# Where kᵀ is turned for two units of a gated linear attention, and when two weight sums are made

## The chip, the cores and the metric

The kernel runs on one core of a Trainium2 chip. The metric is the device time in microseconds of one execution. Its engines are TensorE (matrix products and transposes), VectorE, ScalarE, GpSimd and SyncE (which only issues DMAs); the profile calls them PE, DVE, ACT, POOL and SP. GpSimd and ScalarE can issue DMAs as well. Each engine works through its own queue in order and waits where an input is not there yet.

## The reference

All data is float32. The attention has 4 batches, 8 heads, 768 positions and 48 values a head; its output goes as rows of 384 into a gated MLP with 1536 hidden values.

```python
f = 1.0 / (1.0 + np.exp(-f_logit))
for t in range(S):
    state = f[:, :, t, :, None] * state + np.einsum('bhd,bhe->bhde', k[:, :, t], v[:, :, t])
    y[:, :, t] = np.einsum('bhd,bhde->bhe', q[:, :, t], state)
x = y.transpose(0, 2, 1, 3).reshape(B * S, H * D)
g = x @ w_gate
out = (g * sigmoid(g) * (x @ w_val)) @ w_out
```

## The kernel before

**Units.** The 768 positions are cut into 6 chunks of 128. A unit is one batch in one chunk; units are numbered chunk by chunk, so units 4 to 7 are chunk 1. `attention(u)` is a generator: it makes one unit in steps, and others call its steps in between their own work. In a unit a backward scan (L620) gives the tails of the products of f, k times the tails is `kT` (L570), a forward scan (L648) gives the gates and q times them is `qT`. Scores are products of `kT` and `qT` (L666), masked on VectorE (L681) into `A`; `A`, `v` and the decayed state give `y` (L702 to L727). The new state needs `dS`, products of `v` with `kt` (L747). `kt` is `kT` turned, positions on the partitions.

**Two ways to load.** Early units load rows and turn them on TensorE (L590). The last two units of chunk 1, units 6 and 7, and all later ones load 32-by-32 squares (`by_squares(u)`, four DMAs an input, L447) into rooms that VectorE transposes (L604 for f, L614 for k, L652 for q). In chunks 0 and 1 the rooms lie over the raw tiles of the early units, one room for each input, and units 6 and 7 fill theirs from GpSimd's queue; later chunks load from SP's. `load_after(u, what)` issues the loads of the next unit as soon as a room is free.

**Two ways to turn kT.** Without `turned`, four TensorE transposes (L670) into PSUM and a ScalarE copy (L679) make `kt`. With it (chunks 3 and 4 before), VectorE transposes `kT` block by block into the k room, called `beside` there (L636), four DMAs write it to a tile in DRAM (L639), and one DMA reads it back in the other order (L677). There is one `kt` tile.

**The MLP.** Chunk 0's MLP is plain (L802 for gate and value, L825 for the down product) with four PSUM banks in turn; VectorE multiplies in L816. Chunk 1's attention is dealt out between its pieces, and joins of w_out and sums of weights on VectorE go in there too. From chunk 1 on the MLP saves products by sums: a hidden triple makes 15 products (L1004) out of weights and sums, with ScalarE copies (L1009) and VectorE sums (L905, L908) behind each, then seven down products (L1103, L1166) with w_out's quarters and three sums of them, `down_sums`, made once.

**What sets the order.** Up to the first pieces of chunk 0's MLP, and from chunk 1's MLP on, the instructions keep the order in which they are written on each engine (`in_order`). In between, in the rest of chunk 0's MLP with chunk 1's attention, the framework's scheduler chooses by the order written and its own estimate of times; only loads of squares on GpSimd are kept in order with each other. From chunk 1's MLP on a planner deals out the rest of the work: each product is deemed to take 0.86 us, and a list `waiting` holds steps with due times. `CHAINS` and `SCORES` give them for attention, `DOWN_SUMS_AT` for the four instructions of `down_weight_sums`, counted from the start of chunk 1's MLP. Steps that are due are written ahead of the next product, in order of their due times. For chunk 2 the second unit's gate transpose is due at 13.2, the first unit's masks at 14, the second unit's at 26.65. A triple is deemed 12.9 long.

The four sums are `ws1 = b12 - b11`, `ws2 = b22 - ws1`, `b12 = b22 - b12` and `ws4 = b21 - ws2`, each 128 x 1152.

Of the kernel before, what the change touches and what calls it, by code (L numbers as in the profile page):

```python
# [290 lines left out]
def short_path(ctx, tc, ident, least, judge, q, k, v, f_logit, moe_w_gate, moe_w_val, moe_w_out, out):  # L291
# [9 lines left out]
    nc = tc.nc  # L301
    B, H, S, D = q.shape
    C = 128
    NCH = S // C
# [11 lines left out]
    SQUARES = 2  # L316
# [84 lines left out]
    def by_squares(u):  # L401
        return u >= SQUARES * B - 2
# [6 lines left out]
    def v_of(u):  # L409
        return vs[u % (NV if units[u][1] < SQUARES else NV // 2)]  # L410
# [20 lines left out]
    def load(u, what="fkqv"):  # L431
        b, c = units[u]
        rows = slice(c * C, (c + 1) * C)
        inputs = dict(f=f_logit, k=k, q=q, v=v)
        for nm in "fqkv" if c >= SQUARES else "fvkq" if by_squares(u) else "fkqv":
            src = inputs[nm]
            if nm not in what:
                continue
            if nm == "v":
                dst = v_of(u)  # L440
            elif not by_squares(u):
                dst = raw[nm][u % NRAW]
            else:
                since = len(traced)
                for n in range(4):
                    at = Q * (1 - n % 2)
                    (nc.sync if c >= SQUARES else nc.gpsimd).dma_start(  # L447
                        out=rooms[nm][Q * n:Q * (n + 1), at:at + HP * RUN].rearrange("t (a e) -> t a e", a=HP),
                        in_=src[b, n // 2::2, rows, :].rearrange("a (t i) d -> t a (i d)", i=NI))
                if c < SQUARES:  # L450
                    by_pool.extend(ins for ins in traced[since:] if ins.engine == mybir.EngineType.Pool)
                    keep_order(by_pool[-5:])
                continue
            nc.sync.dma_start(out=dst[:, :, 0:D], in_=src[b, :, rows, :].rearrange("h t d -> t h d"))

    def weight_piece(dst, src, parts):

# [80 lines left out]
    def rows_of(par):  # L538
        return slice(W * par, W * par + D)
# [15 lines left out]
    def attention(u):  # L555
        b, c = units[u]
# [5 lines left out]
        in_squares = by_squares(u)  # L562
# [42 lines left out]
            load_after(u, "f")  # L605
        yield

        turned = SQUARES < c < NCH - 1
        kT = att.tile([128, HP, C], FP32, tag="kT", name="kT")
        qT = att.tile([128, HP, C], FP32, tag="qT", name="qT", bufs=2)  # L610
        kp, qp = kT, qT
# [13 lines left out]
        if not in_squares:  # L625
            kp = transposed("kTp", kr)
            qp = transposed("qTp", qr)
            if by_squares(u + 1):
                load(u + 1)
        multiply(kT, kp, pairs(tail, 2)[:, :, 0:C])  # L630
        yield
        if turned:


            beside = rooms["k"][:, 0:HP * C].rearrange("p (i m) -> p i m", i=NI)
            nc.vector.transpose(beside.rearrange("p i (a e) -> p a i e", e=Q), kT.rearrange("p a (i e) -> p a i e", e=Q))  # L636
            turn = turn_pool.tile([Q, NI, HP, NI, Q], FP32, tag="turn", name="turn")
            for r in range(NI):
                nc.sync.dma_start(out=turn[:, :, :, r, :].rearrange("t i a e -> t (i a) e"),  # L639
                                  in_=beside[Q * r:Q * (r + 1)].rearrange("t i (a e) -> t (i a) e", e=Q))  # L640
            load_after(u, "k")
        yield
# [20 lines left out]
        for a in range(HP):  # L663
            for par in range(2):
                r = rows_of(par)
# [8 lines left out]
        if c < NCH - 1:  # L674
            kt = att.tile([128, HP * C], FP32, tag="kt", name="kt")
            if turned:
                nc.sync.dma_start(out=kt, in_=turn.rearrange("t i a r e -> i t (a r e)"))  # L677
            else:
                nc.scalar.copy(kt, p)  # L679
        for par in range(2):  # L680
# [9 lines left out]
        if c and b < B - 1:  # L690
# [8 lines left out]
            for a in range(HP):  # L699
                for par in range(2):  # L700
                    r = rows_of(par)
# [9 lines left out]
            for h in range(H):  # L711
                a, par = h // 2, h % 2
                f = h * D
                while f < (h + 1) * D:
                    n = min((h + 1) * D, (f // 128 + 1) * 128) - f
                    r = W * (a % 2) + f - h * D
                    (nc.gpsimd if c >= SQUARES else nc.sync).dma_start(out=xT[c][f % 128:f % 128 + n, f // 128, b * C:(b + 1) * C],  # L717
                                                                       in_=yT[r:r + n, par, a // 2 * C:(a // 2 + 1) * C])
                    f += n
        else:  # L720
# [15 lines left out]
            for par in range(2):  # L736
                for n in range(DM // Q):
                    h = n // per * 2 + par
# [11 lines left out]
        if c >= SQUARES and u + 2 < len(units):  # L750
            load(u + 2, "v")
# [7 lines left out]
    def load_after(u, what):  # L759

        if u + 1 < len(units) and u + 1 != SQUARES * B:
            load(u + 1, what)

    def attention_steps(c):

        runs = [attention(c * B + b) for b in range(B)]
        order = sorted((2 * b + s, b, n) for b in range(B)
                       for s, n in enumerate((1, 8, 3, 3) if by_squares(c * B + b) else (3, 6, 3, 3)))
        return [lambda b=b, n=n: [next(runs[b]) for _ in range(n)] for _, b, n in order]
# [9 lines left out]
    def keep_order(mine):  # L779
        for a, b in zip(mine, mine[1:]):  # L780
            tc.add_manual_dep(b, a.name, mybir.DependencyInfo(mybir.DependencyClass.NoSync,
                                                              mybir.DependencyReason.DATA), reason="order")
# [115 lines left out]
        return {"o": banks_o, "A": banks_a}[kind].tile([128, 512], FP32, tag=kind, name="sc")  # L898

    FINISH = (3, 5, 6, 7, 9, 10)  # L900
    DOWN_SUMS_AT = (28, 34, 38, 48)
    sums = {}

    def plus(dst, a, b):
# [31 lines left out]
    def down_weight_sums():  # L936

        DH = DM // 2
        b11, b12 = w_out[:, 0:NP, 0:DH], w_out[:, 0:NP, DH:DM]
        b21, b22 = w_out[:, NP:NF, 0:DH], w_out[:, NP:NF, DH:DM]  # L940
        for i in (1, 2, 4):
            down_sums[i] = comb.tile([128, NP, DH], FP32, tag=f"ws{i}", name=f"ws{i}")
        return [lambda: minus(down_sums[1], b12, b11), lambda: minus(down_sums[2], b22, down_sums[1]),
                lambda: minus(b12, b22, b12), lambda: minus(down_sums[4], b21, down_sums[2])]
# [268 lines left out]
    mark = traced[-1]  # L1213
    keep_warm(5)
    first = [attention(b) for b in range(B)]
    done = [0] * B

# [83 lines left out]
    for c in range(2, NCH):  # L1301
        for b in range(B):
            run = attention(c * B + b)
            waiting += [((c - 2) * whole + t, lambda run=run: next(run)) for t in times(c)[b]]
# [4 lines left out]

    waiting += [(at, f) for at, f in zip(DOWN_SUMS_AT, down_weight_sums())]  # L1310
    blocks = {}
# [26 lines left out]
def kernel(  # L1338
# [22 lines left out]
    def judge(bank):  # L1361
# [13 lines left out]
        yield  # L1375

    short_path(tc, ident, least, judge, *args)
    with tc.If(redo[0] > 0, label="redo"):
        general_path(tc, *args)
# [32 lines left out]
```

## Time and profile before

| | |
|---|---|
| median of 3 runs | 604.13 us (604.05 to 604.21) |
| profiled execution | 605.36 us, span of its instructions 603.5 |
| granted TensorE clock | 0.995 |
| L670, transposes of kT on TensorE | 48 in 12 units, 0.27 us each, overlapping |
| L679, their copies on ScalarE | 12, 0.585 us each |
| L636, VectorE's transposes of kT | 8, 0.703 us each |
| L639 and L677, DMAs of the turn, on SP | 32 of 64 KB, 0.626 us to issue, 2.2 to landing; 8 of 256 KB, 0.568 to issue |
| L447, squares on GpSimd | 24 of 96 KB, 0.55 us to issue |
| L454, v of units 5 to 7 on SP | 192 KB each, 0.47 us to issue, 2.7 to landing |
| L908, sums of w_out's quarters | 4 in all, 1.34 us each |

The span runs from the first to the last instruction. A duration in the profile is that of one instruction; instructions of one engine overlap a little, so from start to start it is shorter. The chain of waits follows the work that ended last back to the beginning. In a timeline a line gives start, duration, engine, source line, operation, output and inputs; in brackets stands the idle time ahead of it and what ended it.

### The profile page before, as it was taken

The page shows a single profiled execution, that of the slowest core. Times are in us where ns is not written, and L with a number is a line of the kernel's source. Part 1 is how long each engine was busy: PE and PEld are TensorE (multiplying, and loading weights), DVE is VectorE, ACT ScalarE, POOL GpSimd, SP SyncE. Part 2 cuts the span into 40 slices and gives each one's busy share as a digit, 9 for nine tenths or more (in the row PEclk, how much of TensorE's full clock was granted, in tenths as well). Part 3 has the DMA queues.
Part 4 walks back from the last instruction along what each step waited for, and adds up shares of the span by engine and source line. Part 5 has one row for each costly group of instructions (what it writes and reads, how often), then busy time and mean ns, then how long its engine had stood idle before and what let it go on. Part 6 is the DMA issues. An engine that isn't in the chain of part 4 may idle for free.

```text
span 603.5 us, 10851 instructions
## 1 busy us (share of the span) xinstructions
PE 591.9 (98%) x4004; PEld 487.6 (81%) x4004; DVE 480.3 (80%) x831; ACT 294.8 (49%) x559; POOL 86.2 (14%) x199
## 2 busy tenths in 40 slices
PE   7899999999999999999999999999999999999996
PEld 5754545667888899888899888899988899988896
DVE  7999997868999977998895978995878982666631
ACT  2577853215776521567631476742376730356600
POOL 1001251000030150030330030330030320000000
PEclk9999999999999999999999999999999999999999
DMA  9998682015322044342434333343240100100001
GB/s 197 243 294 286 199 211 63 5 35 157 80 63 69 17 129 124 102 114 65 115 103 109 116 91 71 87 110 101 85 105 26 28 9 6 53 1 1 1 1 55
DMA packets 105210, 56.28 MB, mean 93 GB/s; under 512 B 67136, under 2 KB 97216, under 8 KB 105152
## 3 DMA queue, kind: packets, MB, share of 16 engines
q1 hardware_dynamic: 97632, 46.49, 29.4%
q0 software_dynamic: 5504, 6.30, 3.5%
q10 hardware_dynamic: 2016, 2.75, 1.3%
q8 instruction: 32, 0.52, 0.4%
q14 instruction: 26, 0.21, 0.1%
HBM read 45.74 MB, written 6.82 MB: 87 GB/s over the span
## 4 chain that ended last, share of the span: by engine, by line
PE 93%; DVE 5%; issue 1%; ACT 0%; DVEq 0%; ACTq 0%
PE o L1103 19%; PE A L1004 16%; PE B L1004 13%; PE c L1004 5%; PE o L1004 5%; PE gate L802 5%; PE o L825 5%; PE val L802 5%; PE sc L666 4%; PE o L1166 3%; PE y L706 3%; PE y L727 2%; PE dS L747 2%; PE y L702 2%; PE kt L670 1%; DVE c L908 1%
## 5 line engine op out<-in xcount | busy, mean ns | idle before, releaser
L717 POOL DMA_DIRECT2D xT<-yT x120 | 59.9, 507 | 50.3 <-ACT yT L710 45.3
L1103 PE MATMUL o<-w_out,h 128*128 128x192 f32 x360 | 62.0, 327 | 0.5 <-DVE h L956 0.5
L1004 PE MATMUL A<-xs,w_both 128*128 128x256 f32 x240 | 62.2, 382 | 0.0
L1103 PEld LDWEIGHTS o<-w_out,h 128*128 128x128 f32 x360 | 58.7, 190 | 1.7 <-DVE h L956 0.8
L1009 ACT COPY c<-A 128x512 f32<-128x512 f32 x40 | 23.3, 583 | 59.5 <-PE A L1004 59.5
L1009 ACT COPY aside<-A 128x512 f32<-128x512 f32 x60 | 35.1, 586 | 33.7 <-PE A L1004 33.6
L905 DVE TENSOR_TENSOR c<-c,aside 128x512 f32<-128x512 f32 x60 | 41.1, 685 | 12.4 <-ACT aside L1009 11.0
L1004 PEld LDWEIGHTS A<-xs,w_both 128*128 128x128 f32 x240 | 44.9, 190 | 6.6
L956 DVE TENSOR_TENSOR h<-h,c 128x256 f32<-128x256 f32 x100 | 40.4, 412 | 7.3 <-ACT h L1020 7.1
L681 DVE TENSOR_TENSOR A<-sc,causal 128x512 f32<-128x512 f32 x48 | 30.9, 686 | 16.9 <-PE sc L666 16.9
L908 DVE TENSOR_TENSOR c<-c,aside 128x512 f32<-128x512 f32 x60 | 40.9, 682 | 2.8 <-ACT aside L1009 2.8
L1020 ACT ACTIVATE h<-c 128x256 f32<-128x256 f32 x100 | 39.2, 416 | 7.6 <-DVE c L905 5.7
L656 POOL MEMSET gates<- 128x4 f32 x24 | 3.3, 139 | 272.6 <-DVE qT L570 267.5
L1103 PE MATMUL o<-ws,h 128*128 128x192 f32 x240 | 41.5, 328 | 0.2 <-DVE A L681 0.2
L1004 PE MATMUL B<-xs,w_both 128*128 128x256 f32 x160 | 41.3, 380 | 0.1
L1004 PE MATMUL c<-xT,w_both 128*128 128x256 f32 x160 | 41.2, 380 | 0.1
L1004 PE MATMUL A<-xs,extra 128*128 128x256 f32 x160 | 41.2, 380 | 0.0
L1004 PE MATMUL B<-xT,extra 128*128 128x256 f32 x160 | 41.1, 379 | 0.0
L1009 ACT COPY aside<-B 128x512 f32<-128x512 f32 x60 | 35.1, 585 | 9.5 <-PE B L1004 6.6
L1103 PEld LDWEIGHTS o<-ws,h 128*128 128x128 f32 x240 | 39.1, 190 | 0.8 <-DVE A L681 0.4
L905 DVE TENSOR_TENSOR c<-c,o 128x384 f32<-128x384 f32 x15 | 8.3, 552 | 36.3 <-PE o L1103 36.3
L908 DVE TENSOR_TENSOR c<-o,c 128x512 f32<-128x512 f32 x40 | 27.4, 684 | 11.0 <-ACT h L1020 6.2
(149 smaller groups left out, 1221.0 us busy)
## 6 DMA issues: line engine op xcount, KB each, us to landing
fsquares<-in_f_logit_dram SPq DMA_DIRECT2D x64, 96.0 KB, 2.5
qsquares<-in_q_dram SPq DMA_DIRECT2D x64, 96.0 KB, 2.1
ksquares<-in_k_dram SPq DMA_DIRECT2D x64, 96.0 KB, 2.4
v<-in_v_dram SPq DMA_DIRECT2D x24, 192.0 KB, 2.7
w<-in_moe_w_gate_dram SPq DMA_DIRECT2D x6, 768.0 KB, 6.1
w<-in_moe_w_val_dram SPq DMA_DIRECT2D x6, 768.0 KB, 6.2
w<-in_moe_w_out_dram SPq DMA_DIRECT2D x6, 768.0 KB, 5.6
out_dram<-ob ACTq DMA_DIRECT2D x14, 192.0 KB, 2.0
```

The lines of the kernel that those rows point to most:

```text
L666: nc.tensor.matmul(sc[par][:, a * C:(a + 1) * C], lhsT=kT[r, a, :], rhs=qT[r, a, :], start=True, stop=True)
L681: nc.vector.tensor_tensor(A[:, par], sc[par].rearrange("p (a t) -> p a t", t=C), causal.unsqueeze(1).broadcast_to((128, HP, C)), ALU.mult)
L717: (nc.gpsimd if c >= SQUARES else nc.sync).dma_start(out=xT[c][f % 128:f % 128 + n, f // 128, b * C:(b + 1) * C], in_=yT[r:r + n, par, a / ...
L802: nc.tensor.matmul(p, lhsT=w[:, j, i, :], rhs=xT[c][:, i, :], start=(i == 0), stop=(i == KT - 1))
L825: nc.tensor.matmul(p, lhsT=hidden_tile(h, n // 2)[:, n % 2 * 2 + b // 2, b % 2 * C:(b % 2 + 1) * C], rhs=w_out[:, j, :], start=(n == 0), s ...
L905: nc.vector.tensor_tensor(dst, a, b, ALU.add)
L908: nc.vector.tensor_tensor(dst, a, b, ALU.subtract)
L956: lagging.append(lambda: f(*args))
L1004: nc.tensor.matmul(p[name][:, n, :], lhsT=weights_of[a][:, n, j, :], rhs=tokens[b], start=fresh and n == 0, stop=True, skip_group_check=True)
L1009: nc.scalar.copy(t, p[name])
L1020: nc.scalar.activation(dst, src[:, 0, :], AF.Silu)
L1103: nc.tensor.matmul(p[:, n, :], lhsT=lhsTs[j][:, n * C:(n + 1) * C], rhs=rhs[:, j, :], start=first and j == order[0] and n == 0, stop=j == ...
```

## The change

It does two things. For units 6 and 7 `kT` is turned by VectorE and DRAM, with the DMAs on GpSimd's queue, in place of TensorE's transposes and ScalarE's copy; as the k room then holds `beside`, unit 7's k loads come after unit 6's turn instead of right after its k transpose. The v loads of units 6 and 7 move from SP's queue to GpSimd's. And the first two of the four sums have other due times: `ws1` 13.1 in place of 28, `ws2` 26.5 in place of 34.

```diff
@@ load
-            nc.sync.dma_start(out=dst[:, :, 0:D], in_=src[b, :, rows, :].rearrange("h t d -> t h d"))
+            queue = nc.gpsimd if c < SQUARES and by_squares(u) else nc.sync
+            queue.dma_start(out=dst[:, :, 0:D], in_=src[b, :, rows, :].rearrange("h t d -> t h d"))
@@ attention
-        turned = SQUARES < c < NCH - 1
+        turned = SQUARES < c < NCH - 1 or c < SQUARES and in_squares
+        turn_queue = nc.sync if c >= SQUARES else nc.gpsimd
...
             for r in range(NI):
-                nc.sync.dma_start(out=turn[:, :, :, r, :].rearrange("t i a e -> t (i a) e"),
+                turn_queue.dma_start(out=turn[:, :, :, r, :].rearrange("t i a e -> t (i a) e"),
                                   in_=beside[Q * r:Q * (r + 1)].rearrange("t i (a e) -> t (i a) e", e=Q))
             load_after(u, "k")
...
             if turned:
-                nc.sync.dma_start(out=kt, in_=turn.rearrange("t i a r e -> i t (a r e)"))
+                turn_queue.dma_start(out=kt, in_=turn.rearrange("t i a r e -> i t (a r e)"))
             else:
                 nc.scalar.copy(kt, p)
@@
-    DOWN_SUMS_AT = (28, 34, 38, 48)
+    DOWN_SUMS_AT = (13.1, 26.5, 38, 48)
```

## The prediction

> **What bounds the kernel now.** I read the busy shares first, then the chain of waits, then the two stretches that the change touches as timelines.
>
> ```profile
> PE 591.9 (98%) x4004; PEld 487.6 (81%) x4004; DVE 480.3 (80%) x831; ACT 294.8 (49%) x559; POOL 86.2 (14%) x199
> PE 93%; DVE 5%; issue 1%; ACT 0%; DVEq 0%; ACTq 0%
> ```
>
> TensorE carries 93% of the chain that ended last, VectorE 5%. So TensorE time taken away inside a stretch in which TensorE never waits shortens the kernel one for one; VectorE time counts only where TensorE waits for it. From 46 to 143 us the waits list names none of TensorE's, and in five windows over 30 to 143 it is busy all the time. There the chain reads:
>
> ```profile
> 106.15 1.09 PE sc L666 x16
> 107.83 5.16 PE o L825 x16
> ...
> 123.56 1.09 PE sc L666 x16
> 125.23 5.16 PE o L825 x16
> ```
>
> The first pair is unit 6 (chunk 1, batch 2), the second unit 7. Scores end at 107.24 and 124.65, the next matmuls begin at 107.83 and 125.23: 0.59 and 0.58 us lie between, and what stands in them in the timeline is four transposes of L670.
>
> The second stretch, 143 to 205 us, is chunk 1's MLP with chunk 2's attention. VectorE's timeline:
>
> ```profile
> 156.41 0.68 DVE L905 TENSOR_TENSOR c<-c,aside 128x512 f32<-128x512 f32 x1
> 157.94 1.12 DVE L604 STREAM_TRANSPOSE gates<-fsquares 128x512 f32<-128x512 f32 x1 [0.84 <-issue]
> ...
> 174.29 1.29 DVE L681 TENSOR_TENSOR A<-sc,causal 128x512 f32<-128x512 f32 x2 [1.41 <-PE sc L666]
> ...
> 176.15 1.35 DVE L908 TENSOR_TENSOR ws<-w_out 128x1152 f32<-128x1152 f32 x1
> ...
> 185.92 1.33 DVE L908 TENSOR_TENSOR ws<-w_out,ws 128x1152 f32<-128x1152 f32 x1
> ```
>
> and TensorE's at its end:
>
> ```profile
> 204.90 1.57 PE L1103 MATMUL o<-w_out,h 128*128 128x192 f32 x8 [0.55 <-DVE h L956]
> ```
>
> VectorE has two idle places, 0.84 us before 157.94 and 1.41 us before 174.29, and none from there to 204. The two sums stand behind the second one. TensorE's 15 products of a triple start every 0.863 us; 30 of them from 174.68 should end at 200.58, and the next work starts at 201.59. So 1.01 us is lost, in steps at 188.91, 195.30 and smaller ones, and 0.55 more at 204.90: at most 1.56 us is to be had.
>
> **What the Trainium skill says.** "DMA: Bandwidth & Descriptors", section "Anatomy of one DMA — SWDGE (gpsimd) path", gives a fixed cost of about 2.0 us for a DMA from GpSimd, most of it the receipt of the write; the trace agrees in size (unit 7's k loads land in 2.4 us, its q loads in 2.9). "Perfetto Trace Analysis", section "Per-instruction lifecycle", says that the slice of such a DMA ends when its descriptors are written, not when data has moved, so a reader must add the landing; the trace agrees (slices of 0.55 us, landings of 2.4). "SBUF — State Buffer", section "SBUF: two separate sides", warns that a VectorE operation in a two-port mode locks GpSimd out of writing descriptors. The trace shows at most a trace of that: one k issue takes 0.71 us where the others take 0.55.
>
> **Part 1, the transposes of units 6 and 7.** Gone: 8 TensorE transposes, 0.59 + 0.58 = 1.17 us, on the path; two ScalarE copies of 0.59 us (L679), worth nothing, since ScalarE was idle 7.7 us before the first and TensorE waits for neither before 117 and 132.
>
> Added on VectorE: two 32-by-32 transposes as L636 (0.70 us, 0.61 from start to start). The first falls in 88 to 107, where VectorE is busy 13.42 of 19 us; the second about 109.7, where it works without a gap until 128.3, but 4.45 us of idleness follow, and the nearest consumers have time (qT of unit 7 is made at 113.55, its scores run at 123.48). Cost nothing. If that cover were gone, 0.61 us each.
>
> Added on GpSimd: two v loads, eight writes to DRAM, two reads back. No row shows such writes from GpSimd. Nearest: xT pieces with 48 runs take 0.504 us, square loads with 128 runs 0.552, so 0.6 ns a run more; a turn's write has 32 x 16 = 512 runs: 0.78 us; a v load has 1024: 1.09. Lower bound 0.55 (the same DMA costs SP 0.63), upper bound all of the square load's time in proportion to runs, 2.2 us a write. I take 0.78, because the two rows show a large fixed part. SP loses two v issues of 0.5 us, behind which nothing waits.
>
> The new wait: kT is now laid into the k room, so unit 7's k loads, issued at 87.75 before, have to wait until the four writes of unit 6 have read it. kT of unit 6 is at 88.22; transpose until 89.5; four issues, 92.6; landed after 2.5 us more, 95.1; four k loads at 0.55, 97.3; landed 99.8. Behind them in GpSimd's queue stand unit 7's q loads and v, the gate reset and unit 6's read back, and in VectorE's queue L614 of unit 7, which ran at 97.79 and would be at 98.4 with the added transpose. It waits 1.4 us. Who waits for it:
>
> ```profile
> 97.79 0.69 DVE L614 STREAM_TRANSPOSE qT<-kraw 128x512 f32<-128x512 f32 x1
> ...
> 98.85 1.23 DVE L648 TENSOR_TENSOR_SCAN gates<-gates,start 128x516 f32<-128x516 f32 x1
> ...
> 101.11 0.69 DVE L816 TENSOR_TENSOR h<-h,val 128x512 f32<-128x512 f32 x1 [1.03 <-PE val L802]
> ...
> 103.68 0.69 DVE L816 TENSOR_TENSOR h<-h,val 128x512 f32<-128x512 f32 x1 [1.89 <-PE val L802]
> ```
>
> From L614's start to the end of the scan it is 2.29 us; the two L816 take 1.29; the second frees the bank that the fourth output of the first down step needs at 103.0 + 3 x 0.645 = 104.94. So L614 may start as late as 104.94 - 3.58 = 101.36 with no loss. At 99.8 there are 1.6 us to spare: cost nothing. The q loads (L652 at 110.29) land by 104; unit 6's kt by 106 for a dS at 117.58; unit 7's kt, which cannot return before that dS ends at 118.2, by 121 for 132.0. All covered.
>
> The order in this stretch is not pinned by hand; the framework's scheduler sets it, and other instructions may change places. I allow 0.5 us either way: part 1 is -1.17, between -0.7 and -1.7.
>
> **Part 2, the two sums.** Due times map to the trace: the first sum at 28 stands at 176.15. Due at 13.1 it precedes the gate transpose due at 13.2 (157.94); due at 26.5 the second precedes the masks due at 26.65 (174.29). A sum takes 1.27 us from start to start. The first starts at 157.01, ends at 158.28, and pushes what follows by 0.34 us; none of ScalarE's copies in that triple is within 0.2 us of waiting for VectorE's release, so TensorE loses nothing (at worst 0.34). The second starts at 173.1 and moves the masks by 0.14, which nobody needs before 206. Then the first removal is worth almost nothing by itself: VectorE would be 1.1 us ahead at 177.5, but its next input comes from a ScalarE copy that ends at 177.31, and the next but two from one that ends at 179.04. It is back in step by 179.1. From there to 204 it does not wait, so the second removal, at 185.92, is worth its 1.27 us: TensorE's waits at 188.91 and 195.30 vanish, the one at 204.90 keeps about 0.3. Part 2 is -1.27, between -0.6 (push paid, half hidden) and -1.56.
>
> **Sum.** -1.17 - 1.27 = -2.44 us. After 205 TensorE waits 0.4 us in all until the end, and no load there is tied to a fixed time, so nothing takes this back. The profiled execution took 605.36 us (span 603.5 and 1.9 around it), the median of the three runs shown is 604.13, 1.2 lower: 605.36 becomes 602.92, and the median 601.7. Own range 600.8 (both parts at their best) to 602.9.
>
> **Rivals.**
> One, the late k: this ends slower. With the upper price of 2.2 us the writes of unit 6 last until 98.3, are landed at 100.8, and unit 7's k is there at 105.5. VectorE stands at L614, TensorE at the fourth output for 4.1 us: -2.44 + 4.1 = +1.7, or 605.8. It decides from L614 at 101.36 on. For it: small runs of 128 bytes, and one first load whose GpSimd slices reach 2.1 us and land in 6.7. Against it: that one ran beside the weight loads, while the DMA share falls to 26% in 88 to 107. Chance 0.13.
>
> Two, part 2 brings nothing: the pushed VectorE work of 157 to 173 holds TensorE for 0.34 and the late stalls stay because ScalarE, not VectorE, ends them. Then -1.17 or less, 603.0. For it, ScalarE copies are named as last in two of the waits; against it, those copies waited for VectorE (188.28, 1.53 us). Chance 0.13.
>
> Three, the removal has no effect because the reshuffled order lets TensorE wait for a read back that the scheduler placed too near, at dS of unit 6 or 7: part 1 becomes a loss of about what it gains, part 2 halves, 604. Chance 0.06.
>
> **How the numbers follow.** The forecast has 0.68. A change of about 0.2%, 1.2 us, is what a measurement here can tell from none: below 602.9 is faster. That is the forecast and some of rival two, 0.73; same is the rest of it and rival three, 0.14; slower is rival one, 0.13. The range from 600.8 to 604.1 takes the forecast and rivals two and three and leaves out rival one and a little on either side.
>
> **What would show it.** Right: no L670 after 90 us in chunk 1, scores of units 6 and 7 followed at once by L825; GpSimd writes near 0.8 us each; L614 of unit 7 between 98.4 and 101.3; the sums just ahead of L604 and L681; L1103 starting about 2.2 us earlier. Wrong: a wait of TensorE near 104 on VectorE, GpSimd writes above 1.5 us, or stalls at the same products of the last triple with VectorE idle before them.

## The result

The changed kernel takes 601.06 us (median of 6 runs, 600.76 to 602.44), the kernel before beside it 604.10 (603.92 to 604.21): ratio 0.9952, with a 95% interval from 0.9942 to 0.9962, or 2.9 us less (3.0 by the medians). The forecast was 601.7, with a range of 600.8 to 604.1.

One caution on the numbers to compare with. The profile that the prediction read was an execution whose granted TensorE clock fell to 0.89 between 20 and 36 us, and everything after it lies more than 1 us late. So the kernel before was profiled once more (label before_again, span 602.2), and positions below are compared with that one. The same window in the first profile and then in the second (length, busy time of PE, PEld, DVE, ACT and POOL, then the granted clock, the DMA share and GB/s):

```profile
20.00:36.00 16.00, 14.21 (x161) 10.19 (x160) 14.81 (x30) 11.05 (x22) 0.30 (x2) 0.89 1.01 280
```

```profile
20.00:36.00 16.00, 14.20 (x164) 9.57 (x163) 15.33 (x30) 11.64 (x23) 0.30 (x2) 1.00 1.01 282
```

The page of the changed kernel (span 599.4), busy shares and chain:

```profile
PE 588.3 (98%) x3996; PEld 485.3 (81%) x3996; DVE 481.8 (80%) x833; ACT 293.5 (49%) x557; POOL 93.8 (16%) x211
PE 97%; DVE 1%; ACT 0%; issue 0%; DVEq 0%; ACTq 0%
```

TensorE has 8 instructions fewer (the transposes), and VectorE's share of the chain is 1% where it was 5%. TensorE's marks, start in us:

| mark | before_again | changed | difference since the mark above |
|---|---|---|---|
| scores of unit 6 | 104.74 | 104.96 | (start: +0.22) |
| unit 6's y from A | 115.31 | 114.59 | -0.94 |
| scores of unit 7 | 122.14 | 121.42 | 0 |
| dS of unit 7 | 130.66 | 129.55 | -0.39 |
| unit 9's first y product, behind the first down products of chunk 1's MLP | 205.06 | 202.66 | -1.29 |
| first down product behind the kernel's last triple | 569.59 | 566.89 | -0.30 |
| end of the span | 602.2 | 599.4 | -0.1 |

The differences behind the first row sum to 3.0 us; less the 0.22 of the first row, 2.8 are left, the difference of the two spans. From 205 to 567 us nothing changes.

**The 0.22 us of the first row** is a price of the v loads. VectorE and TensorE in before_again, then GpSimd, VectorE and TensorE in the changed kernel:

```profile
25.67 0.36 DVE L498 TENSOR_SCALAR top<-top 128x384 int32<-128x384 int32 x1
27.82 1.21 PE L727 MATMUL y<-A,v 128*32 128x128 f32 x32 [0.64 <-issue]
```

```profile
24.94 1.15 POOL L455 DMA_DIRECT2D v<-in_v_dram  x1 [4.50 <-PE dS L749]
25.65 0.60 DVE L499 TENSOR_SCALAR top<-top 128x384 int32<-128x384 int32 x1
28.04 1.21 PE L729 MATMUL y<-A,v 128*32 128x128 f32 x32 [0.89 <-ACT kt L681]
```

While GpSimd issues the v load, a VectorE instruction takes 0.60 us instead of 0.36. The mask behind it starts at 27.26 instead of 27.03, and TensorE's y product, which reads that mask, comes 0.22 later. (The bracket names ScalarE's `kt`, which this product doesn't read.) In v_only (below) the same instruction takes 0.60 us, in turn_only, where v stays on SP, 0.36. The second v load, at 30.17, meets another such instruction at 30.60, which takes 0.63 us; in v_only that load starts at 31.35, and the instruction, at 30.62, takes 0.36. So the longer time goes with the issue on GpSimd that runs beside it.

**First stretch.** The chain of waits of before_again (start, duration, what), and that of the changed kernel:

```profile
102.23 2.58 PE o L825 x8
104.81 1.09 PE sc L666 x16
105.90 0.59 PE kt L670 x4
106.49 5.16 PE o L825 x16
111.65 0.36 PE y L702 x2
112.01 2.78 PE o L825 x8
114.79 0.59 PE y L702 x14
```

```profile
105.03 1.09 PE sc L668 x16
106.12 7.94 PE o L827 x24
114.06 0.60 PE y L704 x16
...
121.49 1.09 PE sc L668 x16
122.58 5.36 PE o L827 x16
```

The scores are followed at once by L827, as said. But look at the runs of down products: 16 of them took 5.16 us behind the transposes and take 5.36 behind the scores. The same 0.20 shows in 8 products of the kernel before: 2.58 behind val's products (at 102.23), 2.78 behind y's (at 112.01). So the products that follow give back 0.20 of each 0.59: a group of transposes is worth 0.39. (The chain counts from the end of what goes before, and the ends of TensorE's instructions are modelled. Counted from start to start, the transposes take 0.49 and the products behind them 0.10 less; the 0.39 is the same.) Behind unit 6 another 0.55 went, because in the changed kernel the scheduler doesn't put two of y's products (x2 at 111.65) ahead of eight down products: 0.36 + 0.59 for y against 0.60, and one 0.20 fewer. 0.39 + 0.55 + 0.39 = 1.33.

**GpSimd in the changed kernel**, its timeline:

```profile
90.32 2.91 POOL L641 DMA_DIRECT2D turn<-kraw  x4 [9.66 <-DVE kraw L638]
93.66 2.25 POOL L447 DMA_DIRECT2D kraw<-in_k_dram  x4 [0.43 <-DMA turn<-kraw]
...
98.10 0.73 POOL L679 DMA_DIRECT2D kt<-turn  x1
```

A write takes 0.65 us (median of 8; four q loads stand in the gap), and k's issue waits only 0.43 us for the last write to land. The last of the k loads lands at about 98.5. VectorE meanwhile:

```profile
99.11 1.23 DVE L650 TENSOR_TENSOR_SCAN gates<-gates,start 128x516 f32<-128x516 f32 x1
100.25 0.69 DVE L616 STREAM_TRANSPOSE qT<-kraw 128x512 f32<-128x512 f32 x1
```

L616 of unit 7 (L614 before) is at 100.25, between 98.4 and 101.3 as expected, but with no idle time ahead of it: k had landed, and the scheduler has put the scan in front. The two L818 behind it run at 100.87 and 102.56, the second after 1.05 us of waiting for TensorE, so nothing is late.

**Second stretch**, VectorE and then the end of TensorE's triple in the changed kernel:

```profile
154.56 1.35 DVE L910 TENSOR_TENSOR ws<-w_out 128x1152 f32<-128x1152 f32 x1
155.83 1.16 DVE L605 STREAM_TRANSPOSE gates<-fsquares 128x512 f32<-128x512 f32 x1
...
170.53 1.37 DVE L910 TENSOR_TENSOR ws<-w_out,ws 128x1152 f32<-128x1152 f32 x1
171.83 1.29 DVE L683 TENSOR_TENSOR A<-sc,causal 128x512 f32<-128x512 f32 x2
...
175.09 0.69 DVE L910 TENSOR_TENSOR c<-o,c 128x512 f32<-128x512 f32 x1 [1.31 <-PE o L1006]
```

```profile
198.40 4.33 PE L1105 MATMUL o<-w_out,h 128*128 128x192 f32 x24
```

Each sum fills an idle place that was there. The first pushes the transpose behind it by about 0.35 us, which TensorE doesn't notice. VectorE is then ahead and waits 1.31 us for TensorE, and the 24 down products run through without the 0.55 us that they waited before. The other gain is in the products ahead of them. Two neighbours in before_again, then in the changed kernel:

```profile
186.43 1.03 PE L1004 MATMUL A<-xs,w_both 128*128 128x256 f32 x4
187.58 1.13 PE L1004 MATMUL B<-xs,w_both 128*128 128x256 f32 x4
```

```profile
185.31 1.03 PE L1006 MATMUL A<-xs,w_both 128*128 128x256 f32 x4
186.18 1.03 PE L1006 MATMUL B<-xs,w_both 128*128 128x256 f32 x4
```

From start to start 1.15 us became 0.87; at 193.97 before, 1.10 became 0.86. From the first of the 30 products to the first down product it was 26.91 us and is 26.18: 0.73 us, and 0.55 at the end, make the 1.28.

### The profile page after: what moved, and what is told of

Its sections match the earlier page's. It is cut to its first block, busy times and chain, and to the rows that moved or that the text cites. A ratio compares the mean times of both kernels' runs of the same rounds, so it can differ in the third digit from the quotient of the medians.

```text
span 599.4 us, 10861 instructions
## 1 busy us (share of the span) xinstructions
PE 588.3 (98%) x3996; PEld 485.3 (81%) x3996; DVE 481.8 (80%) x833; ACT 293.5 (49%) x557; POOL 93.8 (16%) x211
## 4 chain that ended last, share of the span: by engine, by line
PE 97%; DVE 1%; ACT 0%; issue 0%; DVEq 0%; ACTq 0%
PE o L1105 20%; PE A L1006 18%; PE B L1006 14%; PE c L1006 6%; PE o L1006 6%; PE o L827 5%; PE gate L804 5%; PE val L804 5%; PE sc L668 4%; PE o L1168 3%; PE y L708 3%; PE y L729 2%; PE dS L749 2%; PE y L704 1%; PE kt L672 1%; PE fTp L591 0%
```

## Experiments

All ratios are to the kernel before, run on the same chip beside them (its medians lie between 604.0 and 604.1).

**The kernel before again.** No edit.

> The kernel before, profiled once more, unchanged. In the profile shown first, the TensorE clock was 0.88 to 0.90 between 20 and 36 us, and chunk 0's MLP began its second product at 34.25 us; in the profile of the changed kernel the clock there was 1.00 and it was 33.13. Theory: that dip belongs to the one execution, so a second profile starts it near 33.1, has a span near 602.3, and all its later times lie 1.1 us earlier. Rival: the early stretch is slower whenever v of units 6 and 7 is loaded from SP; then it is 34.2 again, at a clock of 1.0.

603.97 us, span 602.2, clock 0.998. So the 1.2 us by which the first profiled execution stood over the median came with that clock and are no property of the kernel.

**The change in its parts.** `turn_only` keeps the old due times and v on SP; `v_only` has nothing but v on GpSimd's queue; `sums_only` is the kernel before with the new due times.

```diff
turn_only, to the changed kernel
-            queue = nc.gpsimd if c < SQUARES and by_squares(u) else nc.sync
+            queue = nc.sync
-    DOWN_SUMS_AT = (13.1, 26.5, 38, 48)
+    DOWN_SUMS_AT = (28, 34, 38, 48)
v_only, to the changed kernel
-        turned = SQUARES < c < NCH - 1 or c < SQUARES and in_squares
+        turned = SQUARES < c < NCH - 1
-    DOWN_SUMS_AT = (13.1, 26.5, 38, 48)
+    DOWN_SUMS_AT = (28, 34, 38, 48)
sums_only, to the kernel before
-    DOWN_SUMS_AT = (28, 34, 38, 48)
+    DOWN_SUMS_AT = (13.1, 26.5, 38, 48)
```

> The turn of kT by VectorE and DRAM on GpSimd's queue alone: v of units 6 and 7 stays on SP, the sums stay due at 28 and 34. Theory: 604.1 - 1.17 for eight transposes, and some 0.2 for two matmuls of L704 that the scheduler no longer splits off: 602.7 (602.4 to 603.0), chunk 1's MLP begins 1.3 us earlier, and the later waits of the last triple (1.0 + 0.5 us) are all still there. Rival: the v loads carry part of the gain; then it is above 603.2.

> Only the v loads of units 6 and 7 on GpSimd's queue, all else as before. Theory: no change, 603.9 to 604.3, as SP's queue sets nothing there. Rival: it takes up to 0.5 us off the first 36 us, where SP's DMA issues follow each other closely: 603.6.

> Only the two due times 13.1 and 26.5. Theory: -1.27 us, 602.8 (602.6 to 603.0): TensorE loses nothing ahead of 174 us and the waits at the second and ninth product of the last triple go. Rival: the two parts need each other, or the first sum holds up TensorE; then -0.6 or less, above 603.5.

| | median us | ratio | 95% interval |
|---|---|---|---|
| turn_only | 602.46 | 0.9975 | 0.9968 to 0.9982 |
| v_only | 603.89 | 0.9993 | 0.9984 to 1.0001 |
| sums_only | 602.85 | 0.998 | 0.9968 to 0.9993 |

The turn brings about 1.6 us and the sums 1.2, together 2.8 of the 2.9; v on GpSimd's queue brings nothing that can be told from none: its 0.22 us at 28 us are there in v_only too, but that profile ends sooner behind TensorE's last product, by 0.4. In the traces turn_only has the first stretch of the changed kernel (scores of unit 6 to y from A 9.63 us, scores of unit 7 to dS 8.13), while v_only and sums_only have that of before (10.57 and 8.52, with y's two products split off). sums_only reaches unit 9's first y product at 203.78 instead of 205.06: 1.28 us.

**One sum or two, and where.**

```diff
-    DOWN_SUMS_AT = (28, 34, 38, 48)
+    DOWN_SUMS_AT = (13.1, 34, 38, 48)        first_sum_only
+    DOWN_SUMS_AT = (13.1, 28, 38, 48)        both_one_slot
```

> The kernel before with due times 13.1 and 34: the first sum leaves its place for the idle place before 157 us, the second stays. Theory: VectorE, freed of the first sum at 176, only waits for ScalarE's copies 3 us later, so this is worth 0 to 0.15 us: 604.0 (603.8 to 604.2). Rival: every sum taken out of 174 to 187 us is worth its 1.27 us; then 602.8, like the two together.

> The kernel before with due times 13.1 and 28: the second sum moves up only as far as the place that the first one had, behind the masks. Theory: that place has slack for one sum, so it costs nothing there, and 185.9 is freed: -1.27 us, 602.8, the same as with 26.5. Rival: the idle place ahead of the masks is needed; then VectorE is late from 176 on and the time is 603.7 or more.

first_sum_only takes 604.0 us, ratio 1.0002 (0.9994 to 1.001); both_one_slot 602.71, ratio 0.998 (0.9972 to 0.9989). The first removal is worth nothing by itself. With the second sum in the first one's old place, the whole 1.3 us is there. Each of the two kernels has one sum left in the stretch from 174 to 187 us, so their number doesn't decide; the place does. VectorE in first_sum_only:

```profile
176.19 0.69 DVE L908 TENSOR_TENSOR c<-o,c 128x512 f32<-128x512 f32 x1 [1.32 <-PE o L1004]
184.57 1.33 DVE L908 TENSOR_TENSOR ws<-w_out,ws 128x1152 f32<-128x1152 f32 x1
```

The time won by the first removal is spent at once, in a wait for TensorE. A sum ahead of 176 is paid out of that wait; the one at 184.57 has no wait of VectorE's behind it before 203, and TensorE pays it. TensorE's waits in first_sum_only (total us, times, longest); both_one_slot has the last two alone:

```profile
PE o L1103 <- DVE h L956: 0.5, 1, 0.5
PE o L1103 <- DVE A L681: 0.2, 1, 0.2
PE A L1004 <- ACT aside L1009: 0.2, 1, 0.2
```

**The writes made three times, in the changed kernel.** This brings about the rival of the late k. The extra writes repeat the same bytes.

```diff
-            for r in range(NI):
+            for r in list(range(NI)) * (1 if c >= SQUARES else 3):
```

> The changed kernel with each of the four DRAM writes of units 6 and 7 issued three times, so that unit 7's k loads come later. Twelve writes of 0.65 us last from 90.3 to 98.1, land at 100.3, k is there at 105. Theory: the price of a late k is set by where VectorE's transpose of it stands in the queue, and the scheduler, which knows of the later writes, puts it behind the two multiplications that free PSUM: no loss, 601.1 (600.8 to 601.5). Rival: VectorE stands at it and TensorE at the fourth down output, for 105 + 1.9 - 103.8 = 3.1 us: 604.2.

608.79 us, ratio 1.0088 (1.0071 to 1.0106): 7.7 more than the changed kernel. No wait of TensorE near 104 us appears; the scheduler had put L616 at 111.91, some 7 us after k had landed. The loss is elsewhere. GpSimd's queue and TensorE's timeline:

```profile
128.78 0.70 POOL L679 DMA_DIRECT2D kt<-turn  x1 [2.03 <-DMA turn<-kraw]
```

```profile
129.98 10.59 PE L827 MATMUL o<-w_out,h 128*128 128x384 f32 x32
140.49 0.67 PE L749 MATMUL dS<-v,kt 128*64 128x48 f32 x16
142.71 1.10 PE L1006 MATMUL A<-xs,w_both 128*128 128x256 f32 x4 [1.55 <-DMA out_dram<-ob]
145.64 1.60 PE L1006 MATMUL B<-xs,w_both 128*128 128x256 f32 x4 [1.82 <-DVE xs L907]
```

Unit 7's kt is read back at 128.78, and dS of unit 7 stands behind all the down products that were left, at 140.49 instead of 129.55. What stands behind it on VectorE, the sums for chunk 1's MLP among it, comes 11 us later, and the first products of that MLP wait for VectorE and an output DMA. So the turn can cost time, and in this trace it does so through the place that the scheduler gives dS, not through the k room. This is read from one trace; no edit moved dS alone.

**The turn's DMAs on SP, in the changed kernel.** `turn_queue = nc.sync`.

> The changed kernel with the ten DMAs of the turn of units 6 and 7 on SP's queue in place of GpSimd's; all else as changed. Theory: the queue is not what matters, since the returned kt is there 13 and 9 us before its use and SP has time between 80 and 130 us: 601.1 (600.8 to 601.5). Rival: SP, in order, waits for the turn to land before it can issue the pieces of xT or weights that stand behind, the next products get their inputs late: 601.8 or more.

601.58 us, ratio 0.9961 (0.9945 to 0.9976), span 599.6, and TensorE's marks are within 0.1 us of the changed kernel's. The intervals of the two ratios overlap widely, so which queue carries the turn makes no difference that can be told from none; both are early enough.

**More units turned, in the changed kernel.** Chunk 2's last unit, 11, and the last two, 10 and 11, turned by VectorE and SP.

```diff
-        turned = SQUARES < c < NCH - 1 or c < SQUARES and in_squares
+        turned = SQUARES < c < NCH - 1 or c < SQUARES and in_squares or u == 11          turn_11
+        turned = SQUARES < c < NCH - 1 or c < SQUARES and in_squares or u in (10, 11)    turn_10_11
```

> The changed kernel with unit 11 (chunk 2, batch 3) turned by VectorE and DRAM as well, on SP's queue. Its kT is made in the down stage of chunk 1, where VectorE is busy 28.4 of 37 us. Theory: TensorE's 0.59 us go and nothing is paid, 600.5 (600.2 to 600.8). Rival: unit 12's k loads have to wait for the turn to be read, VectorE waits for them and so do the down sums behind: 601.1 or more.

> Units 10 and 11 both turned so. Unit 10's kT is made about 182 us, in the triples, where VectorE works without a gap from 175 to 200. Theory: TensorE gains 1.18 us, but VectorE's 0.61 us more come back as a wait of about 0.5 at the end of the last triple: 600.4. Rival: VectorE still has that slack now that the sum at 185.9 is gone, all 1.18 us stay: 599.9.

turn_11: 601.44 us, ratio 0.9959 (0.9944 to 0.9973), no gain over the changed kernel. TensorE in the changed kernel, then in turn_11:

```profile
217.39 0.66 PE L672 MATMUL kt<-idf,kT 128*128 128x128 f32 x4
218.23 4.17 PE L1105 MATMUL o<-ws,h 128*128 128x192 f32 x24 [0.19 <-DVE A L683]
```

```profile
216.35 1.16 PE L668 MATMUL sc<-qT,kT 48*128 48x128 f32 x16
218.29 4.17 PE L1105 MATMUL o<-ws,h 128*128 128x192 f32 x24 [0.78 <-DVE A L683]
```

Here the next products wait for VectorE's masks of the same scores, the first of which is done at 218.2 in both. The transposes stood in that wait; without them the wait is longer by 0.59.

turn_10_11: 601.8 us, ratio 0.9968 (0.9958 to 0.9978). Unit 10's transposes do bring 0.39 (from the scores of unit 10 to the next y product 9.09 us instead of 9.48). But VectorE's transpose of unit 10 falls into the triple that ends at 203, where VectorE is the limit, and the 0.55 us wait is back:

```profile
201.96 1.57 PE L1105 MATMUL o<-w_out,h 128*128 128x192 f32 x8 [0.55 <-DVE h L958]
```

The next y product starts at 203.45 instead of 202.66: 0.79 lost, 0.39 gained, 0.40 worse at unit 11's scores (216.69 against 216.29).

**The last 0.3 us.** At the end of the kernel's last triple a ScalarE copy starts late in the kernel before, and a product of TensorE's waits for it. The timeline of ScalarE in before_again, then in the changed kernel:

```profile
567.99 0.58 ACT L1009 COPY aside<-A 128x512 f32<-128x512 f32 x1 [1.50 <-PE A L1004]
```

```profile
565.29 0.58 ACT L1011 COPY aside<-A 128x512 f32<-128x512 f32 x1 [1.20 <-PE A L1006]
```

Its idle time is 1.49 or 1.50 us in all five kernels that leave units 6 and 7 to TensorE, and 1.19 or 1.20 in all eight that turn them on VectorE. In all eight TensorE gains 0.30 us there. Without added copies they have at least two ScalarE copies fewer. Two kernels put two back, small ones: `two_scalar_copies` beside the removed ones (a table load came with them, 560 instructions on ScalarE), and `two_scalar_more` in a way that leaves the count as it was before, 559.

```diff
two_scalar_copies
+            if turned and c < SQUARES:
+                idle = att.tile([128, 4], FP32, tag="idle", name="idle")
+                nc.scalar.copy(idle, causal[:, 0:4])
two_scalar_more
+    idle = const.tile([128, 2, 4], FP32, tag="idle", name="idle")
...
+            if turned and u == 7:
+                for i in range(2):
+                    nc.scalar.copy(idle[:, i], least[:, 4, :])
```

> The changed kernel with two ScalarE copies of 128 x 4 put in early, where ScalarE has time, so that its instruction count is that of the kernel before. With the turn alone the execution is 0.3 us shorter after 205 us too; in the three profiles that still have the two copies the last triple's copy of A starts 0.27 us late (idle 1.50 us before it), in the two without it does not (1.20). Theory: it goes by ScalarE's count of instructions, so the 0.27 us comes back: 601.35, and the copy is late again. Rival: it has to do with what is done, not with the count; then 601.06 and no late copy.

> The changed kernel with two ScalarE copies of 128 x 4 put in early that bring no table load with them, so that every later ScalarE instruction has the same number as in the kernel before (in the earlier try a table load came along, and the numbers were three higher in place of two). Theory: the late start of the last triple's copy of A goes by the number of the instruction, so ScalarE is idle 1.50 us before it again. Rival: it stays at 1.20.

601.18 us, ratio 0.9956 (0.9943 to 0.9968), and 601.43 (one run). The idle time stays at 1.20 and 1.19. So neither the number of ScalarE's instructions nor their numbering is the cause. What the cause is stays open; that the 0.30 goes with the turn, and not with the sums or v, is what the runs show. The rest, 0.1 to 0.2 us behind TensorE's last product, differs from profile to profile (0.4 in v_only) and is not explained either.

## Why the prediction was right

**Part 1, the transposes.** Right in sign and place, two terms mis-sized. The 0.59 and 0.58 were read off the gap between scores and down products; the step that fails is taking the gap for the price, since the down products behind take 0.20 us more without transposes ahead of them. Each group is worth 0.39, in the chain above and again for unit 10. What was missing is the 0.55 of y's two products that are no longer split off, which is about the 0.5 that was allowed either way for changed places. Hence 1.33 where 1.17 stood: 0.39 too much and 0.55 too little, and that the two nearly cancel is luck. The 0.30 at the kernel's last triple was not seen at all.

**Part 1, the costs.** The cover held: no wait of TensorE's between 46 and 205 us is listed. A write on GpSimd took 0.65 us, between the bounds and under the 0.78 taken. The wait of 1.4 us at L614 didn't come: k landed at about 98.5 instead of 99.8, and the scan took L614's place. The read back of unit 6 was issued at 98.10 and landed 5.8 us later, at 103.9, still long before dS at 115.51. The Trainium skill ("DMA: Bandwidth & Descriptors", section "Anatomy of one DMA — SWDGE (gpsimd) path") gives about 2.0 us of fixed cost: the writes' landing of 2.3 agrees in size. The read back of 256 KB took over 3 us more than that; whether its size or its many small runs are behind this, no run here separates. One reading was off without effect: in the first profile VectorE does wait between 109.7 and 128.3 us, 0.84 us before 123.59.

The v loads are the cost that was put at nothing and was not. They took 1.15 and 0.90 us (estimate 1.09), but at 24.94 and 30.17 us, where the scheduler put them, and not behind unit 7's k. The prediction asked only whether VectorE holds up a DMA's issue on GpSimd; at 25.65 it was the VectorE instruction that took longer, and 0.22 us of TensorE's time were lost.

**Part 2.** Right in its mechanism: 1.28 us for 1.27, the first removal nothing (604.0), the second all, VectorE ahead and waiting at 175, the 0.55 us gone. The shares were off, again in both directions. About 0.3 of the wait at the end was to stay, and none did; the steps in the products were to go, 1.01 us, and 0.73 of them did.

**The rivals.** The late k didn't come, and with the writes tripled it did no harm where it was looked for: k landed at about 104.7, L616 was simply put later, and no wait for k came. What cost 7.7 us there is close to the third rival, a dS and its read back, at several times the size given there; only that TensorE didn't stand at dS, but dS was put behind all the down products. Rival two falls with sums_only (0.9968 to 0.9993).

**The total.** By the profiles +0.22 for v, -1.33, -1.28, -0.30 at the kernel's last triple and 0.1 to 0.2 at the very end make -2.8 to -2.9, against -2.44. The forecast lay 0.6 us above the measured median, inside its range, and it came as near as that only because errors of both signs met.

## What to carry to other kernels

The price of a removed group of TensorE instructions is read over the instructions that follow as well: compare the same successor (here the runs of down products) behind different predecessors in the trace before. It is worth that price only where nothing else is waited for there: the same transposes brought 0.39 us in one unit and nothing in another, where a mask ended the wait anyway. VectorE work is moved for gain out of a stretch behind which VectorE does not wait any more until TensorE needs it, and into a place where it does wait; a move out of a place that has such a wait right behind it brought nothing (604.0). And a DMA that moves to GpSimd's queue can cost VectorE time beside it, 0.24 us for one instruction here, so look at what VectorE does while it is issued.

## What the runs showed of the hardware

A DMA write from GpSimd with 512 runs of 128 bytes took 0.65 us to issue, SP 0.63 for the same. With the 1024 runs of a v load GpSimd was the slower one: 1.15 and 0.90 us, against 0.43 to 0.63 for the last three v loads of before_again on SP. Beside such an issue a VectorE TENSOR_SCALAR of 128x384 took 0.60 to 0.63 us instead of 0.36. The read back of 256 KB landed after 5.5 to 5.8 us, the writes of 64 KB after 2.3 (median). In some executions of several of these kernels the granted clock is 0.88 to 0.90 between 20 and 36 us (also in those profiled of turn_only and v_only), and all that follows lies 1.1 to 1.4 us later: a single profile is no measure of a change of this size. And an identical ScalarE copy near the end started about 0.3 us later or earlier with changes made 450 us before it, for a reason that the runs did not find.
